# In the experts' first tile, the next tile's tokens are rounded behind the second weights, and the next first-layer weights behind the last part of the first layer

## The chip, the cores and the metric

The kernel runs on one core of a Trainium2 chip. The metric is device time in microseconds of one execution; the lowest is best. The kernel before was timed three times.

A core has five engines that work side by side, each through its own queue of instructions in order: PE (matrix multiplication; its weight loads are shown as PEld), DVE (vector work), ACT (activations, copies and casts), POOL (general work, and the issue of scatters) and SP, which here only issues loads. An instruction waits in its queue until what it needs is there, and everything behind it waits too.

## The reference

Attention over 8 batches of 8 heads, 576 tokens and head size 64, with a decay and a causal mask, and then a layer of 8 experts of which each token takes one:

```python
def _moe_ref(x, modality_id, w_gate, modality_bias, w1, w2):
    logits = x @ w_gate + modality_bias[modality_id]     # x: attention's output, 4608 x 512
    e_idx = np.argmax(logits, axis=1)
    ...                                                  # gate_w: the softmax weight of that expert
    for e in range(E):                                   # 8 experts
        mask = e_idx == e
        h = np.maximum(x[mask] @ w1[e], 0.0)             # 512 -> 1024
        out[mask] = gate_w[mask, None] * (h @ w2[e])     # 1024 -> 512
```

Everything is float32.

## The kernel before

**Attention** takes the first 395 us. It goes through the batches, and for each batch of tokens it works out the expert of each token and scatters its rows into per-expert lists in memory (`xs`); the scatters are issued by POOL (L769), five for each batch. The last batch's scatters are issued while the experts have already begun.

**The experts** (`Moe.run`) work through tiles of 256 tokens of one expert. To keep float32's accuracy, every operand of a matmul is split into a rounded part and the rest: ACT casts to the rounded part (names ending in h), and DVE subtracts it to get the rest (names ending in l). A product is then three matmuls: h with h, h with l, l with h. One tile has these steps:

- `load_x` (L1084): SP loads the tokens `xg` of tile t + 2. A load of tokens waits for all scatters recorded so far.
- `load_w1`, `load_w2`: SP loads raw weights of the next tile's expert into `raw1` and `raw2`. They are conditional: if the next tile has the same expert, nothing is moved.
- `split_w2`: four pieces of `w2h` (ACT, L1135) and `w2l` (DVE, L1136).
- `first` (L1160): the first layer in four groups of 24 matmuls, each into one PSUM bank `ph` of three; after each group ACT writes `hh` (L1171) and DVE `hl` (L1172).
- `split_w1`: four pieces of `w1h` (ACT, L1116) and `w1l` (DVE, L1118) of the next tile's weights. The q-th piece may only be overwritten when the q-th group of the first layer is done.
- `prepare` (L1143): PE transposes the next tile's `xg` in two halves into PSUM banks `px0` and `px1`; ACT casts to `xh` (L1155), DVE makes `xl` (L1156).
- `second` (L1180): the second layer, 24 matmuls for each half of the tokens, into `py0` and `py1`; DVE multiplies by the gate into `y` (L1190), and POOL scatters `y` to the output (L1191).

In what follows, a ph matmul is one of the first layer (128 x 128 by 128 x 256) and a py matmul one of the second (128 x 128 by 128 x 512).

After the first tile (`t == OTHERS`, which is 1), `other_tables` and `pads` run once: PE sums the counts of tokens (L971 and L1076, two small matmuls into `px0`), DVE copies them (`c_nb`, L975) and works out the tables of the remaining tiles, POOL writes padding rows (L1081).

**The order of the work.** A scheduler with its own model of durations places the instructions of the expert part on each engine; the program text only gives dependencies. In the first tile, which overlaps with the last of attention, some orders are fixed by hand: `self.order(x, behind)` says that instruction x stands behind another on its engine, without a wait. `follow(behind, x, y)` does so for a pair: x, an ACT instruction, behind `behind[0]`, and y, on DVE, behind `behind[1]`; it returns the pair's own names for the next. `split_w2` returns the four pairs of names (`w2h`, `w2l`); so `behind[3]` in `body` is the last pair. With `behind=None` nothing is fixed. After the last piece of w1 was ordered, the scheduler decides where the rest stands, on PE too, where no order is fixed by the lines that change.

Of the kernel before, what the change touches and what calls it, by code (L numbers as in the profile page):

```python
# [18 lines left out]
AF = mybir.ActivationFunctionType  # L19
# [41 lines left out]
def f32(ap):  # L61
    return ap.bitcast(F32)
# [132 lines left out]
class Attn:  # L195
# [303 lines left out]
    def max_mm(self, p, g):  # L499
        nc = self.nc  # L500
        X = self.get("X", p)
        self.owned(("cum", p % 3), p)
        pm = self.new(self.ps_s, "ps", ("m", p, g), [P, 2, 512], F32, 3)
        segs = self.SEG[g]
        masked = [s for s in segs if s[3] + s[1] == MW[s[2]]]
        first = True
        for c0, w, ic, j0 in masked:
            for x, n in ((0, P), (1, 64)) if w > 64 else ((1, 64),):
                for h in range(2):
                    r = slice(64 * h, 64 * h + 64)  # L510
                    nc.tensor.matmul(pm[:, h, c0 + w - n:c0 + w], self.id2[r, x], self.after[r, x, P - n:], start=first, stop=False,
                                     skip_group_check=True)
                first = False
        for c0, w, ic, j0 in segs:
            for h in range(2):
                r = slice(64 * h, 64 * h + 64)
                nc.tensor.matmul(pm[:, h, c0:c0 + w], self.Cq[r], self.Sk[r, p % 3, j0:j0 + w], start=not masked, stop=False,
                                 skip_group_check=True)
        for c0, w, ic, j0 in segs:
            for h in range(2):  # L520
                r = slice(64 * h, 64 * h + 64)
                nc.tensor.matmul(pm[:, h, c0:c0 + w], X[r, 0, QC - 64 + P * ic:QC + 64 + P * ic], X[r, 0, j0:j0 + w],
                                 start=False, stop=True, skip_group_check=True)
# [39 lines left out]
    def scores(self, p, g):  # L563
        nc = self.nc
        X = self.get("X", p)
        self.owned(("cum", p % 3), p)
        self.owned(("shift", p % 3), p)
        self.owned(("lo", p % 3), p)
        ps = self.new(self.ps_s, "ps", (p, g), [P, 2, 512], F32, 3)
        segs = self.KSEG[g]  # L570
        masked = [s for s in segs if s[3] == P * s[2]]
        first = True
        for c0, w, c, i0 in masked:
            for x, n in ((1, P), (0, 64)) if w > 64 else ((0, 64),):
                for h in range(2):
                    r = slice(64 * h, 64 * h + 64)
                    nc.tensor.matmul(ps[:, h, c0:c0 + n], self.id2[r, x], self.later[r, x, 0:n], start=first, stop=False,
                                     skip_group_check=True)
                first = False
        for c0, w, c, i0 in segs:  # L580
            k = slice(KC + P * c, KC + P * c + P)
            for h in range(2):
                r = slice(64 * h, 64 * h + 64)
                nc.tensor.matmul(ps[:, h, c0:c0 + w], self.Sk[r, p % 3, k], self.Sq[r, p % 3, 64 + i0:64 + i0 + w],
                                 start=not masked, stop=False, skip_group_check=True)
        for c0, w, c, i0 in segs:
            k = slice(KC + P * c, KC + P * c + P)
            q = slice(QC + i0, QC + i0 + w)
            for j, (x, y) in enumerate(((0, 0), (0, 1), (1, 0))):
                for h in range(2):  # L590
                    r = slice(64 * h, 64 * h + 64)
                    nc.tensor.matmul(ps[:, h, c0:c0 + w], X[r, x, k], X[r, y, q], start=False, stop=(j == 2), skip_group_check=True)  # L592
# [286 lines left out]
    def run(self, early=None):  # L879
        self.own("acc", -1)  # L880
        with self.tc.manual_schedule():
            self.setup(*self.begin)
            for s in self.steps(early).order():
                s["fn"]()
# [19 lines left out]
class Moe:  # L904
# [238 lines left out]
    def prepare(self, t, behind=None):  # L1143

        nc = self.nc
        xg = self.xg[t]
        xh = self.next("xh")
        xl = self.next("xl")
        self.xh[t], self.xl[t] = xh, xl
        for c in range(2):  # L1150
            px = (self.px(c) if t or c == 0 else self.next("ph")).rearrange("p (k n) -> p k n", n=P)
            for k in range(4):
                nc.tensor.transpose(px[:, k, :], xg[:, c, k * P:k * P + P], self.ident)
            a = xh[:, :, c * P:c * P + P]
            x = nc.scalar.copy(a, px)  # L1155
            y = nc.vector.tensor_tensor(xl[:, :, c * P:c * P + P], px, f32(a), ALU.subtract)  # L1156
            behind = self.follow(behind, x, y)
        return behind

    def first(self, t, ranks=None, behind=()):  # L1160
        nc = self.nc
        xh, xl = self.xh[t], self.xl[t]
        for g in range(4):
            ph = self.next("ph").rearrange("p (a n) -> p a n", a=2)
            for i in range(2):
                f0 = (2 * g + i) * P
                m = [(k, w, x) for k in range(4) for w, x in ((self.w1h, xh), (self.w1h, xl), (self.w1l, xh))]
                for j, (k, w, x) in enumerate(m):
                    y = nc.tensor.matmul(ph[:, i, :], w[:, k, f0:f0 + P], x[:, k, :], start=(j == 0), stop=(j == len(m) - 1))  # L1169
            a = self.hh[:, 2 * g:2 * g + 2, :]  # L1170
            nc.scalar.activation(a, ph, AF.Relu)  # L1171
            z = nc.vector.scalar_tensor_tensor(self.hl[:, 2 * g:2 * g + 2, :], ph, 0.0, f32(a), ALU.max, ALU.subtract)  # L1172
            if ranks:
                self.order(z, ranks[1] if g == 0 else behind[g - 1][1])
                if g:
                    self.order(behind[g][2], z.ins.name)
            if ranks and g == 2:
                self.order(ranks[0], y.ins.name)
# [60 lines left out]
    def run(self, acc, loads, behind, ahead, ranks):  # L1239
        self.load_w1(self.row[0], 0, loads)  # L1240
        self.load_w2()
        behind = self.split_w1(0, [0], behind, (0, 2))
        behind = self.prepare(0, behind)
        for x in ahead:
            self.order(x, behind[1])
        self.split_w1(0, [1, 2, 3], behind, (0, 2))
        self.nc.gpsimd.memset(self.raw1[1], 0.0)
        nest = ExitStack()
        for t in range(FULL):
            if t == OTHERS:  # L1250
                self.other_tables(self.counts(acc, self.px(0), "b", self.half_way))
                self.pads(acc)

            def body():
                self.load_w1(self.row[t + 1])
                if t + 2 < FULL:
                    self.load_x(t + 2)
                behind = self.split_w2(None if t else ranks)
                self.load_w2()
                self.first(t, None if t else ranks, behind)  # L1260
                self.split_w1(0, behind=None if t else behind[3])
                if t + 1 < FULL:
                    self.prepare(t + 1)
                half = self.second(self.xg[t], 2)
                if t == 0:
                    self.half_way = half
            if t == ALWAYS:
                every = ()
                nt = self.val(self.row[EARLY], 3, FULL - EARLY, ALWAYS - EARLY, every)
                nh = self.val(self.rowh[0], 3, 8, 0, every)  # L1270
                for h in range(2):
                    self.load_xh(h)
                self.prepare_h(0)
            if t >= ALWAYS:
                nest.enter_context(self.tc.If(nt > t - EARLY))
            body()
        nest.close()
        with ExitStack() as nest:  # L1278
            for t in range(8):
                nest.enter_context(self.tc.If(nh > t))  # L1280
                self.half(t)
# [85 lines left out]
```

## Time and profile before

| | |
|---|---|
| time, median of 3 runs | 873.17 us (872.64 to 876.27) |
| the profiled execution | 874.83 us, span of its instructions 873.0 us |
| mean granted PE clock | 0.989 |
| busy share of the span | PE 93%, PEld 84%, DVE 74%, ACT 60%, POOL 42% |
| attention | until about 395 us |
| the experts' first tile (t = 0) | about 382 to 420 us, overlapping with attention's end |
| tiles after that | some 23 us each |

The span is the time from the first to the last instruction on the core. In a row of the order of time stand the start, the duration, the engine, the line, the operation, what it writes and reads, and in brackets how long the engine had been idle and what ended that. In a row of the waits stand the waiting engine, its line, what it waited for, and then the sum in us, the number of waits, and the longest.

### The profile page before, as it was taken

How to read it: one execution, taken by the hardware profiler on the slowest of the kernel's cores; microseconds unless marked ns; L12 is line 12 of the kernel's file. 1: busy time of each engine (PE TensorE's matmuls, PEld its weight loads, DVE VectorE, ACT ScalarE, POOL GpSimd, SP SyncE). 2: the span in 40 equal slices, each digit the busy share in tenths (PEclk: the TensorE clock that was granted, in tenths of full speed). 3: DMA queues.
4: the chain of work that ended last, by engine and by line, in shares of the span. 5: the costliest groups of instructions: out<-in, count | busy, mean ns of one | idle time of the engine just before them, and what ended most of it. 6: DMA issues, size and time to landing. Idle time of an engine off the chain costs nothing. (4 is left out here: it accounts for less than half of the span.)

```text
span 873.0 us, 23522 instructions
## 1 busy us (share of the span) xinstructions
PE 814.1 (93%) x9702; PEld 731.2 (84%) x9702; DVE 649.2 (74%) x1214; ACT 521.3 (60%) x640; POOL 370.9 (42%) x346
## 2 busy tenths in 40 slices
PE   4899999999999999896999999999999999999894
PEld 3689888888888888785999999999999999999673
DVE  7789899999999999867876666666666656666394
ACT  3587777878787878564455445454445435455382
POOL 8366778888888888674510111111101100111010
PEclk9999999999999999999999999999999999999997
DMA  5334344444444443262267621101114321134650
GB/s 195 132 113 142 120 142 140 147 141 138 139 139 143 140 147 99 69 233 83 97 233 283 231 75 49 48 28 47 37 49 145 133 65 49 49 113 172 225 220 23
DMA packets 43301, 108.50 MB, mean 124 GB/s; under 512 B 5423, under 2 KB 5615, under 8 KB 43184
## 3 DMA queue, kind: packets, MB, share of 16 engines
q1 hardware_dynamic: 36480, 85.87, 29.5%
q0 software_dynamic: 6704, 21.02, 6.4%
q8 instruction: 79, 1.29, 0.6%
q14 instruction: 38, 0.31, 0.1%
HBM read 144.19 MB, written 21.80 MB: 190 GB/s over the span
## 5 line engine op out<-in xcount | busy, mean ns | idle before, releaser
L1191 POOL DMA_INDIRECT out_dram<-y,xg x36 | 45.8, 1272 | 352.4 <-DVE y L1190 335.2
L1169 PE MATMUL ph<-xh,w1h 128*128 128x256 f32 x576 | 163.1, 283 | 0.0
L1169 PE MATMUL ph<-xl,w1h 128*128 128x256 f32 x576 | 162.9, 283 | 0.0
L1169 PE MATMUL ph<-xh,w1l 128*128 128x256 f32 x576 | 162.9, 283 | 0.0
L1135 ACT CAST w2h<-raw 128x1024 fp32r<-128x1024 f32 x84 | 86.3, 1048 | 117.9 <-issue 57.4
L634 POOL TENSOR_TENSOR Pl<-Pt,Ph 128x1024 f16<-128x1024 f32 (+1 forms) x63 | 141.5, 2259 | 5.7 <-ACT Ph L622 5.3
L1136 DVE TENSOR_TENSOR w2l<-raw,w2h 128x1024 fp32r<-128x1024 f32 x84 | 100.5, 1220 | 52.2 <-ACT w2h L1135 50.8
L1118 DVE TENSOR_TENSOR w1l<-raw,w1h 128x1024 fp32r<-128x1024 f32 x78 | 96.1, 1240 | 56.9 <-ACT w1h L1116 56.5
L1116 ACT CAST w1h<-raw 128x1024 fp32r<-128x1024 f32 x80 | 83.0, 1048 | 90.3 <-PE ph L1169 67.1
L1186 PE MATMUL py<-w2l,hh 128*128 128x512 f32 x312 | 119.7, 393 | 2.7 <-DVE w2l L1136 2.7
L1186 PE MATMUL py<-w2h,hh 128*128 128x512 f32 x312 | 121.1, 397 | 0.0
L1186 PE MATMUL py<-w2h,hl 128*128 128x512 f32 x312 | 119.7, 392 | 0.0
L378 POOL TENSOR_TENSOR X<-raw,X 128x1216 fp32r<-128x1216 f32 x31 | 85.9, 2772 | 63.7 <-ACT X L372 60.6
L1169 PEld LDWEIGHTS ph<-xl,w1h 128*128 128x128 f32 x576 | 110.4, 192 | 0.8
L1169 PEld LDWEIGHTS ph<-xh,w1h 128*128 128x128 f32 x576 | 110.4, 192 | 0.7
L1169 PEld LDWEIGHTS ph<-xh,w1l 128*128 128x128 f32 x576 | 110.4, 192 | 0.0
L592 PE MATMUL ps<-X 64*128 64x288 f32 (+4 forms) x1152 | 106.9, 316 | 0.0
L660 PE MATMUL po<-vh,Ph 128*128 128x73 f16 x930 | 100.1, 198 | 6.4 <-DVE lgh L676 3.3
L607 ACT ACTIVATE Pt<-ps,lnp 128x576 f32<-128x576 f32 (+1 forms) x96 | 79.6, 866 | 43.6 <-PE ps L592 42.6
L660 PEld LDWEIGHTS <-Ph 128*128 128x128 f16 x960 | 93.7, 98 | 10.5 <-DVE lgh L676 4.7
L662 PE MATMUL po<-vh,Pl 128*128 128x73 f16 x930 | 99.8, 197 | 0.3 <-issue 0.3
L661 PE MATMUL po<-vl,Ph 128*128 128x72 f16 x930 | 99.9, 196 | 0.0
(285 smaller groups left out, 1888.7 us busy)
## 6 DMA issues: line engine op xcount, KB each, us to landing
raw<-in_w_dram SPq DMA_DIRECT2D x84, 1024.0 KB
raw<-in_qk_dram SPq DMA_DIRECT2D x32, 608.0 KB
xg<-xs SPq DMA_DIRECT2D x20, 514.0 KB
vT<-in_vt_dram SPq DMA_DIRECT2D x32, 320.0 KB
vr<-in_v_dram SPq DMA_DIRECT2D x30, 256.0 KB
raw1b<-in_w_dram SPq DMA_DIRECT2D x4, 1024.0 KB
hxg<-xs SPq DMA_DIRECT2D x5, 257.0 KB
vr<-in_v_dram SPq DMA_DIRECT2D x8, 128.0 KB
```

The source lines that it names most:

```text
L378: e.tensor_tensor(X[:, 1], self.get("raw", p), f32(X[:, 0]), ALU.subtract)
L592: nc.tensor.matmul(ps[:, h, c0:c0 + w], X[r, x, k], X[r, y, q], start=False, stop=(j == 2), skip_group_check=True)
L634: e.tensor_tensor(self.Pl_t[p % 2][:, :, c], self.exps(p, i), self.Ph_t[p % 2][:, :, c], ALU.subtract)
L660: nc.tensor.matmul(o, Ph[:, c0:c0 + P], vh[:, c, hh, :], start=(c == 0), stop=False)
L661: nc.tensor.matmul(o[:, 1:73], Ph[:, c0:c0 + P], vl[:, c, hh, :], start=False, stop=False)
L662: nc.tensor.matmul(o, Pl[:, c0:c0 + P], vh[:, c, hh, :], start=False, stop=(c == ic))
L1116: x = nc.scalar.copy(self.w1h[a], self.raw1[i][a])
L1118: y = e.tensor_tensor(self.w1l[a], self.raw1[i][a], f32(self.w1h[a]), ALU.subtract)
L1135: x = nc.scalar.copy(self.w2h[a], self.raw2[a])
L1136: y = nc.vector.tensor_tensor(self.w2l[a], self.raw2[a], f32(self.w2h[a]), ALU.subtract)
L1169: y = nc.tensor.matmul(ph[:, i, :], w[:, k, f0:f0 + P], x[:, k, :], start=(j == 0), stop=(j == len(m) - 1))
L1186: x = nc.tensor.matmul(py, h[:, k, c * P:c * P + P], w[:, k, :], start=(j == 0), stop=(j == len(m) - 1))
```

## The change

Three lines. In `prepare`, an order given by hand is applied to both halves of a tile's tokens only for tile 0; for another tile only to the second half (c = 1). `first` keeps the name of its last activation (`relu`). And in the body of the first tile, `split_w1` is ordered on ACT behind that activation instead of behind the last `w2h` cast (on DVE behind the last `w2l` as before), and `prepare` of tile 1, which had no order by hand, gets one: its second half stands behind the last `w2h` on ACT and behind the second `w2l` on DVE. For all later tiles nothing is said, as before.

```diff
             x = nc.scalar.copy(a, px)
             y = nc.vector.tensor_tensor(xl[:, :, c * P:c * P + P], px, f32(a), ALU.subtract)
-            behind = self.follow(behind, x, y)
+            if t == 0 or c == 1:
+                behind = self.follow(behind, x, y)
         return behind
...
             a = self.hh[:, 2 * g:2 * g + 2, :]
-            nc.scalar.activation(a, ph, AF.Relu)
+            self.relu = nc.scalar.activation(a, ph, AF.Relu).ins.name
...
                 self.first(t, None if t else ranks, behind)
-                self.split_w1(0, behind=None if t else behind[3])
+                self.split_w1(0, behind=None if t else (self.relu, behind[3][1]))
                 if t + 1 < FULL:
-                    self.prepare(t + 1)
+                    self.prepare(t + 1, None if t else (behind[3][0], behind[1][1]))
```

The scheduler's result differs on PE, DVE and ACT from the first tile on; the queues of POOL and SP are the same. One line is added, so that line numbers behind L1156 are one higher with the change. Names carry buffer numbers: `ph0` to `ph2` are the banks of the first layer, `py0` and `py1` of the second, `px00` and `px10` of the transposes, and `xh1`, `xl1` belong to tile 1.

**DVE**, first tile, after the last of attention's routing. Before:

```order
L738 TENSOR_REDUCE rr1_9328<-rrk_9324 128x5
L1156 TENSOR_TENSOR xl1_9409<-px10_9380,xh1_9407 128x4x128
L1136 TENSOR_TENSOR w2l_9435<-raw2_9399,w2h_9431 128x1024
L1172 SCALAR_TENSOR_TENSOR hl_9427<-ph2_9371,hh_9423 128x512
L1136 TENSOR_TENSOR w2l_9435<-raw2_9399,w2h_9431 128x1024
L1172 SCALAR_TENSOR_TENSOR hl_9427<-ph0_9369,hh_9423 128x512
L1136 TENSOR_TENSOR w2l_9435<-raw2_9399,w2h_9431 128x1024
L1172 SCALAR_TENSOR_TENSOR hl_9427<-ph1_9370,hh_9423 128x512
L1136 TENSOR_TENSOR w2l_9435<-raw2_9399,w2h_9431 128x1024
L1118 TENSOR_TENSOR w1l_9392<-raw1_9384,w1h_9388 128x4x256 x4
L1136 TENSOR_TENSOR w2l_9435<-raw2_9399,w2h_9431 128x1024
```

and with the change, from the fourth w2l on:

```order
L1136 TENSOR_TENSOR w2l_9435<-raw2_9399,w2h_9431 128x1024
L1118 TENSOR_TENSOR w1l_9392<-raw1_9384,w1h_9388 128x4x256 x4
L1156 TENSOR_TENSOR xl1_9409<-px10_9380,xh1_9407 128x4x128
L1136 TENSOR_TENSOR w2l_9435<-raw2_9399,w2h_9431 128x1024 x2
L1191 TENSOR_SCALAR y0_9410<-py0_9375,xg0_78 128x512
L1136 TENSOR_TENSOR w2l_9435<-raw2_9399,w2h_9431 128x1024
L1191 TENSOR_SCALAR y1_9411<-py1_9376,xg0_78 128x512
L975 COPY c_nb_9674<-px00_9365 1x8
```

The second half of tile 1's xl has moved from ahead of the first w2l to behind the four w1l; the first w2l follows the routing's reduction (L738) at once. What stands between, w2l and hl by turns, is unchanged.

**ACT**, at the same place, from the first tile's four w2h on. Before:

```order
L1135 CAST w2h_9431<-raw2_9399 128x1024 x4
L1116 CAST w1h_9388<-raw1_9384 128x4x256 x2
L1171 ACTIVATE hh_9423<-ph0_9369 128x512
L1155 CAST xh1_9407<-px10_9380 128x4x128
L1116 CAST w1h_9388<-raw1_9384 128x4x256 x2
L1171 ACTIVATE hh_9423<-ph1_9370 128x512
```

and with the change:

```order
L1135 CAST w2h_9431<-raw2_9399 128x1024 x4
L1172 ACTIVATE hh_9423<-ph0_9369 128x512
L1155 CAST xh1_9407<-px10_9380 128x4x128
L1172 ACTIVATE hh_9423<-ph1_9370 128x512
L1116 CAST w1h_9388<-raw1_9384 128x4x256 x4
L1135 CAST w2h_9431<-raw2_9399 128x1024 x4
```

All four w1h stand behind the last hh of the first layer, and xh1 two casts earlier.

**PE**, in the second layer of tile 0. Before, the transposes of tile 2's tokens (xg2) stand there, behind two matmuls of tile 1:

```order
L1186 MATMUL py1_9376<-w2h_9431,hh_9423 128x512
L1169 MATMUL ph2_9371<-xh1_9407,w1h_9388 128x256
L1169 MATMUL ph2_9371<-xl1_9409,w1h_9388 128x256
L1153 MATMUL px10_9380<-cident_61,xg2_80 128x128 x4
L1186 MATMUL py0_9375<-w2l_9435,hh_9423 128x512
L1186 MATMUL py0_9375<-w2h_9431,hl_9427 128x512
```

With the change xl1 is first used behind the whole second layer of tile 0 and the first count matmul:

```order
L1187 MATMUL py1_9376<-w2h_9431,hl_9427 128x512
L971 LDWEIGHTS cones_66
L971 MATMUL px00_9365<-c_acc_9347,cones_66 128x8
L1170 MATMUL ph1_9370<-xh1_9407,w1h_9388 128x256
L1170 MATMUL ph2_9371<-xl1_9409,w1h_9388 128x256
L1170 MATMUL ph2_9371<-xh1_9407,w1l_9392 128x256
```

and the first transpose of xg2 ahead of the last group of tile 1's first layer:

```order
L1170 MATMUL ph1_9370<-xh1_9407,w1h_9388 128x256
L1170 MATMUL ph1_9370<-xl1_9409,w1h_9388 128x256
L1170 MATMUL ph1_9370<-xh1_9407,w1l_9392 128x256
L1153 MATMUL px10_9380<-cident_61,xg2_80 128x128
L1170 MATMUL ph2_9371<-xh1_9407,w1h_9388 128x256
L1170 MATMUL ph2_9371<-xl1_9409,w1h_9388 128x256
```

The other three transposes of that half stand behind that group, after the four of the first half. The second count matmul (L1076) stands 37 ph matmuls behind the first use of xl1, and the transposes of xg2 32 more.

## The prediction

> **What bounds the kernel now.** I read the profile in this order: busy time by stretch, the waits of the matmul engine, then the order of time around each wait. First the stretches round the hand-over from attention to the experts (columns: stretch, length, then PE, PEld, DVE, ACT, POOL busy, granted clock, DMA share, GB/s).
>
> ```profile
> 400.00:410.00 10.00, 3.52 (x16) 2.79 (x17) 10.00 (x11) 3.15 (x4) 7.15 (x6) 1.00 0.43 159
> 410.00:420.00 10.00, 10.00 (x42) 8.06 (x41) 5.46 (x7) 2.85 (x4) 1.00 (x1) 0.83 0.06 26
> 420.00:440.00 20.00, 20.00 (x136) 18.49 (x136) 16.23 (x65) 7.54 (x10) 11.27 (x9) 1.00 0.31 119
> 440.00:500.00 60.00, 60.00 (x407) 55.72 (x406) 39.94 (x43) 31.42 (x38) 6.79 (x6) 1.00 0.70 251
> ```
>
> From 410 to 500 PE is never idle, and DVE, ACT and DMA have room: the expert part runs at PE's pace, so PE time lost at its start goes straight into the end. It loses some: only 3.52 of the 10 us before 410, and a granted clock of 0.83 in the next 10. Two of PE's waits lie there.
>
> ```profile
> PE px L1153 <- DMA xg<-xs: 4.9, 1, 4.9
> PE py L1186 <- DVE w2l L1136: 2.7, 1, 2.7
> ```
>
> In order of time (start, duration, instruction), with the rows that give the pace between them:
>
> ```profile
> 398.49 0.28 PE L1169 MATMUL ph<-xl,w1h 128*128 128x256 f32 x1
> 398.61 0.28 PE L1169 MATMUL ph<-xh,w1l 128*128 128x256 f32 x1
> 401.62 0.50 PE L1186 MATMUL py<-w2l,hh 128*128 128x512 f32 x1 [2.73 <-DVE w2l L1136]
> 401.96 0.39 PE L1186 MATMUL py<-w2h,hl 128*128 128x512 f32 x1
> ...
> 404.62 0.28 PE L1169 MATMUL ph<-xl,w1h 128*128 128x256 f32 x1
> 409.76 0.78 PE L1153 MATMUL px<-cident,xg 128*128 128x128 f32 x4 [4.86 <-DMA xg<-xs]
> 410.19 0.78 PE L1186 MATMUL py<-w2l,hh 128*128 128x512 f32 x1
> ...
> 413.67 0.39 PE L1186 MATMUL py<-w2l,hh 128*128 128x512 f32 x1
> 413.90 0.39 PE L1186 MATMUL py<-w2h,hl 128*128 128x512 f32 x1
> ```
>
> Starts count here, as matmuls overlap: a ph matmul takes 0.12 us (398.49 to 398.61), a py matmul 0.23 (413.67 to 413.90). After the second wait eight py matmuls take 3.48 us (410.19 to 413.67).
>
> **What the change takes away.** In tile 0 the second half of tile 1's rounding (xh, then xl) no longer stands ahead of the first w2l on DVE, and ACT casts w1h only after the whole first layer. The scheduler's PE order follows: xl of tile 1 and the transposes of tile 2's tokens (xg) come later.
>
> First wait. DVE's side of it:
>
> ```profile
> 396.19 0.20 DVE L738 TENSOR_REDUCE rr<-rrk 128x5 f32<-128x40 f32 x1
> 399.75 0.69 DVE L1156 TENSOR_TENSOR xl<-px,xh 128x512 fp32r<-128x512 f32 x1 [3.36 <-ACT xh L1155]
> 400.36 1.22 DVE L1136 TENSOR_TENSOR w2l<-raw,w2h 128x1024 fp32r<-128x1024 f32 x1
> 401.49 0.68 DVE L1172 SCALAR_TENSOR_TENSOR hl<-ph,hh 128x512 fp32r<-128x512 f32 x1
> 402.09 1.22 DVE L1136 TENSOR_TENSOR w2l<-raw,w2h 128x1024 fp32r<-128x1024 f32 x1
> ...
> 406.69 4.62 DVE L1118 TENSOR_TENSOR w1l<-raw,w1h 128x1024 fp32r<-128x1024 f32 x4
> 420.70 0.75 DVE L1190 TENSOR_SCALAR y<-py,xg 128x512 f32<-128x512 f32 x1
> 421.36 0.14 DVE L975 COPY c_nb<-px 1x8 f32<-1x8 f32 x1
> ```
>
> DVE stands idle 3.36 us for xh, which ACT does late; PE waits for the w2l behind it. With xl gone from there w2l can start at 396.4 and end at 397.6, before PE asks at 398.73 (398.61 + 0.12). PE gains 401.62 - 398.73 = 2.89, and 0.11 of a slow first interval (401.62 to 401.96 is 0.34 instead of 0.23): 3.00 us.
>
> Second wait. PE asks for xg's transposes at 404.74 and starts at 409.76: 5.02 us. In the new order 34 py matmuls and much of tile 1's first layer stand ahead of them. The eight slow matmuls go with the wait: 3.48 - 8 x 0.23 = 1.64. The sum is 3.00 + 5.02 + 1.64 = 9.66 us.
>
> **Whether the work ahead is ready.** The new PE clock, counted from 398.73: 12 py (2.76) to 401.5, one ph, 12 py to 404.4, one ph, 22 py (5.06) to 409.6, one count matmul and one ph, xl first used at 409.7, 37 ph (4.44) to the second count matmul at 414.2, 32 ph (3.84) to the first transpose of xg at 418.0. Against it ACT and DVE, from these rows and those above:
>
> ```profile
> 394.86 1.99 ACT L1135 CAST w2h<-raw 128x1024 fp32r<-128x1024 f32 x2
> 396.75 2.00 ACT L1116 CAST w1h<-raw 128x1024 fp32r<-128x1024 f32 x2
> 398.65 0.59 ACT L1171 ACTIVATE hh<-ph 128x512 fp32r<-128x512 f32 x1
> 399.14 0.58 ACT L1155 CAST xh<-px 128x512 fp32r<-128x512 f32 x1
> 399.60 2.00 ACT L1116 CAST w1h<-raw 128x1024 fp32r<-128x1024 f32 x2
> 407.32 1.05 ACT L1135 CAST w2h<-raw 128x1024 fp32r<-128x1024 f32 x1 [5.21 <-DMA raw<-in_w_dram]
> ```
>
> - ACT: hh at 396.75, xh to 397.7, then hh of the last group when PE ends it at 398.9, to 399.5; four w1h at 0.95 each end at 403.4. The first, done at 400.6, is wanted at 401.5; the second (401.5) at 404.4; the third (402.4) at 409.6. So the later w1h is hidden, by 0.9 us at the narrowest.
> - DVE: w2l (1.13) and hl (0.60) by turns from 396.4 to 402.7, always ahead of their matmuls; four w1l (4.6) to 407.3; xl to 407.9, wanted at 409.7: 1.8 us to spare.
> - Behind xl in DVE's queue stand tile 1's w2l, y, the count copy c_nb, and hl. w2l waits for ACT's w2h, whose wait ends at 407.32 as before: two casts to 409.2, a third, once py1's fifth of eleven is done at 408.5, to 410.2. DVE: two w2l from 408.4 to 410.7, y (0.66) to 411.3, w2l to 412.5, y to 413.1, c_nb to 413.25; the second count matmul wants that at 414.2: 0.9 us to spare. The next hl frees a bank of PSUM for PE's group at 418.0: ACT's w1h after the ph group that ends at 412.5 is done at 413.7, DVE's last w2l and six small copies (0.08 each) end at 414.9, w1l at 416.0, two small ones and hl at 416.9: 1.1 us to spare.
> - The tokens xg land unchanged before 409.76; wanted at 418.0.
>
> That 407.32 hangs on POOL and SP, where nothing is moved:
>
> ```profile
> 381.15 0.91 POOL L769 DMA_INDIRECT xs<-x,rde  x1 [0.21 <-issue]
> ...
> 406.44 3.52 POOL L1247 MEMSET raw1b<- 128x4096 f32 x1 [2.29 <-DMA xs<-x,rde]
> 406.45 0.36 SPq L1089 DMA_DIRECT2D xg<-xs  x1
> 407.16 0.51 SPq L1110 DMA_DIRECT2D raw<-in_w_dram  x2
> ```
>
> The last scatter of tokens lands at 406.44; SP then loads xg and issues raw at 407.16, and ACT starts 0.16 us later, so that load is skipped (tile 1 has tile 0's expert). Then DVE's queue can't run ahead of the scatters, and the slack of 0.9 us is all there is.
>
> **Costs that the trace doesn't show.** Splitting xg's transposes into two pieces on PE: between 0 and 0.1 us (the transposes' whole stretch was 0.43, 409.76 to 410.19); I take 0.06. The first w2l's real readiness is hidden behind xl: somewhere from below 396.4 to 400.36. Beside raw it waits, as the program has it, for five scatters of the seventh image, the last issued at 381.15; with the landing of 2.29 us above that is 384.4, so I take 396.4; the other end costs 3.0 us. DVE beside POOL:
>
> ```profile
> 385.28 2.97 POOL L1118 TENSOR_TENSOR w1l<-raw,w1h 128x1024 fp32r<-128x1024 f32 x1 [0.50 <-ACT w1h L1116]
> 386.77 2.56 DVE L1118 TENSOR_TENSOR w1l<-raw,w1h 128x1024 fp32r<-128x1024 f32 x1
> ```
>
> A w1l of DVE took 2.56 instead of 1.22 beside such an operation of POOL, +1.34. Now four w2l shift onto POOL's scatters and xl, w2l onto its memset. The price is between 0 (w2l at 400.36 and 402.09 took 1.22 during scatters, four w1l at 406.69 took 4.62 during the memset) and 4 x 1.34 = 5.4 us of DVE. I take 0, as those rows are the same pair of operations. Nothing here can gain: PE does the same matmuls.
>
> [...]
>
> So the span goes from 873.0 to 873.0 - 9.6 = 863.4. The profiled execution took 874.83, 1.83 more than its span, and lies above the median of 873.17; from the median I forecast **863.5 us**.
>
> **Rivals.**
> 1. *A new wait on DVE takes part of it back.* If the four w2l run beside POOL at 2.56, DVE is 5.4 us late, xl ends at 413.3, and PE waits 3.6 at 409.7, a gap longer than the 2.73 that left the clock alone, shorter than the 4.86 that didn't. With the slow matmuls (1.64) 5.2 is lost: 868.7; for smaller stretches, beyond 0.9 us of slack, 864 to 867. [...]
> 2. *The first w2l isn't ready.* It would start at 400.36 as now: 3.0 us less, 866.5. For it: its own wait was never seen. Against: 384.4.
> 3. *The loads take it back.* From 440 the queue moves 251 GB/s; if loads set the pace there, tiles 3 on would not start earlier, and the time stays at 873.
>
> ```profile
> SPq L1097 <- DVE w1l L1118: 25.2, 10, 5.4
> ACT w1h L1116 <- DMA raw<-in_w_dram: 0.2, 1, 0.2
> ```
>    Against: from 330 to 560 SP's weight loads wait for DVE, and after 440 ACT waits for a load 0.2 us in all: loads follow compute.
> 4. *Slower: xl at the end of DVE's queue.* If all eight operations ahead of it (four w2l, four w1l) ran at 2.56, xl would end 10.7 us late, at 418.6; PE would stand 8.9 us at 409.7 and pay 1.64: 873.17 - 9.6 + 10.5 = 874.1. It decides from xl ending at 417.7. Against: the 4.62 for four w1l.
>
> **Chances.** Forecast 0.73; rival 1 0.13; rival 2 0.06; rival 3 0.05; rival 4 0.03. About 0.5% (4.4 us) is what a measurement tells from no change. The forecast, rival 2 and most of rival 1 are beyond it: faster 0.91; rival 3 and rival 1's extreme within: 0.06; slower 0.03. The range: 862.0, since the lowest of the runs shown (872.64) less 9.66 is 863.0 and a microsecond is left for scatter; up to 868.7 with rival 1's extreme.
>
> **What would show it.** Right: w2l starts near 396.5 without a wait; PE has no wait over 0.5 us from 398 to 440 and the granted clock of that stretch is 1.00; the first transposes of xg start near 418; the count copy ends near 413. Wrong: a PE wait for xl, c_nb or hl between 409 and 419 (rival 1 or 4), w2l starting near 400 (rival 2), or ACT waiting for raw after 430 with PE idle (rival 3).

## The result, and the profile after

The changed kernel took **869.23 us** (median of 11 runs, 865.85 to 872.75); the kernel before, run beside it, 875.35 us (11 runs, 870.88 to 878.74). The ratio is 0.9937, with a 95% interval of 0.991 to 0.9963: faster by 5.5 us by that ratio, where 9.6 were forecast. The forecast of 863.5 is not reached, and 869.23 lies above the upper end of the range, 868.7. A part of that distance is the kernel before, which took 2.2 us more here than the 873.17 from which the forecast started; the gain itself fell short all the same.

The profiled execution took 870.31 us, with a span of 868.6 against 873.0. First the stretches after the hand-over, and PE's waits from 396 to 500 (columns as in the prediction):

```profile
400.00:410.00 10.00, 10.00 (x47) 8.03 (x46) 8.46 (x9) 3.72 (x4) 7.84 (x9) 1.00 0.34 119
410.00:420.00 10.00, 6.81 (x51) 6.70 (x51) 6.98 (x14) 5.51 (x7) 5.26 (x2) 0.91 0.23 80
420.00:440.00 20.00, 20.00 (x120) 18.08 (x120) 15.36 (x59) 7.07 (x10) 11.09 (x10) 0.96 0.37 128
```

```profile
PE px L1076 <- DVE c_nb L975: 3.2, 1, 3.2
```

The stretch from 400 to 410, where PE was busy for 3.52 us before, is full now, at clock 1.00. Both waits of the prediction are gone. But a new one stands between 410 and 420, and the clock falls behind it. In order of time on PE:

```profile
414.48 0.28 PE L1170 MATMUL ph<-xh,w1l 128*128 128x256 f32 x1
417.95 0.17 PE L1076 MATMUL px<-c_acc,cones 128*128 128x8 f16 x1 [3.19 <-DVE c_nb L975]
...
418.30 0.41 PE L1170 MATMUL ph<-xh,w1l 128*128 128x256 f32 x1
...
421.50 0.37 PE L1170 MATMUL ph<-xh,w1h 128*128 128x256 f32 x1
```

PE could have gone on at 414.60 (414.48 + 0.12) and does at 417.95: 3.35 us. From 418.30 to 421.50 lie 15 ph matmuls at 0.213 us instead of 0.12: 1.40 us. Lost together: 4.75 of the 9.66 that were to be won, which leaves 4.9.

That sum can be held against the trace without what varies elsewhere. I measure the **expert part** on PE: from the matmul L724 of the last routing to the end of the last full tile, which is the start of the first half tile's matmul (L1223 before, L1224 after) less the idle time in its bracket.

```profile
395.65 0.18 PE L724 MATMUL pb<-acc,ones 128*128 128x40 f16 x1
...
818.76 0.47 PE L1223 MATMUL ph<-w1h,hxh 128*128 128x512 f32 x1 [2.86 <-issue]
```

```profile
396.06 0.18 PE L724 MATMUL pb<-acc,ones 128*128 128x40 f16 x1
...
814.44 0.76 PE L1224 MATMUL ph<-w1h,hxh 128*128 128x512 f32 x1 [2.97 <-PEq L1278]
```

Before: 818.76 - 2.86 - 395.65 = 420.25. After: 814.44 - 2.97 - 396.06 = 415.41. That is 4.84 less, against 4.9 from the sum. So the three terms of the forecast came together as predicted, and a new wait took half of them back.

Where that wait comes from is read on POOL. Its scatters and the small operation ahead of them, before and then after (start, duration):

```profile
396.54 0.20 POOL L742 TENSOR_TENSOR re<-re,rr 128x5 f32<-128x5 f32 x1 [1.38 <-DVE rr L738]
397.47 0.98 POOL L769 DMA_INDIRECT xs<-x,rde  x1 [0.32 <-POOL between L768]
398.76 1.01 POOL L769 DMA_INDIRECT xs<-x,rde  x1 [0.22 <-issue]
400.07 0.97 POOL L769 DMA_INDIRECT xs<-x,rde  x1 [0.21 <-issue]
401.35 1.06 POOL L769 DMA_INDIRECT xs<-x,rde  x1 [0.22 <-issue]
402.72 1.43 POOL L769 DMA_INDIRECT xs<-x,rde  x1 [0.22 <-issue]
```

```profile
396.94 1.24 POOL L742 TENSOR_TENSOR re<-re,rr 128x5 f32<-128x5 f32 x1 [1.38 <-DVE rr L738]
398.86 1.85 POOL L769 DMA_INDIRECT xs<-x,rde  x1 [0.27 <-POOL between L768]
401.02 1.45 POOL L769 DMA_INDIRECT xs<-x,rde  x1 [0.21 <-issue]
402.78 1.39 POOL L769 DMA_INDIRECT xs<-x,rde  x1 [0.21 <-issue]
404.47 1.97 POOL L769 DMA_INDIRECT xs<-x,rde  x1 [0.21 <-issue]
406.75 1.97 POOL L769 DMA_INDIRECT xs<-x,rde  x1 [0.23 <-DMA xs<-x,rde]
```

The five scatters take 8.63 us instead of 5.45, and L742 takes 1.24 instead of 0.20: 4.22 us more in a row. What follows them is late by that and by 0.40, by which attention's routing ended later in this execution (L724 at 396.06 instead of 395.65). SP and ACT after:

```profile
411.09 0.36 SPq L1089 DMA_DIRECT2D xg<-xs  x1
411.79 0.51 SPq L1110 DMA_DIRECT2D raw<-in_w_dram  x2
```

```profile
411.94 3.89 ACT L1135 CAST w2h<-raw 128x1024 fp32r<-128x1024 f32 x4 [8.23 <-DMA raw<-in_w_dram]
```

SP issues xg at 411.09 instead of 406.45, 4.64 later, and raw behind it. ACT's w2h, to which the prediction gave 407.32, waits 8.23 us and starts at 411.94. Then DVE:

```profile
396.90 1.23 DVE L1136 TENSOR_TENSOR w2l<-raw,w2h 128x1024 fp32r<-128x1024 f32 x1
398.04 0.68 DVE L1173 SCALAR_TENSOR_TENSOR hl<-ph,hh 128x512 fp32r<-128x512 f32 x1
398.64 1.22 DVE L1136 TENSOR_TENSOR w2l<-raw,w2h 128x1024 fp32r<-128x1024 f32 x1
...
403.24 4.62 DVE L1118 TENSOR_TENSOR w1l<-raw,w1h 128x1024 fp32r<-128x1024 f32 x4
407.78 0.68 DVE L1156 TENSOR_TENSOR xl<-px,xh 128x512 fp32r<-128x512 f32 x1
413.02 2.36 DVE L1136 TENSOR_TENSOR w2l<-raw,w2h 128x1024 fp32r<-128x1024 f32 x2 [4.56 <-ACT w2h L1135]
...
417.75 0.14 DVE L975 COPY c_nb<-px 1x8 f32<-1x8 f32 x1
```

DVE itself is not slowed: w2l 1.22, four w1l 4.62, xl done at 408.5 with time to spare, all as predicted. It then stands idle for 4.56 us behind tile 1's w2l, and the count copy c_nb ends at 417.89 instead of 413.25.

### The profile page after: what moved, and what is told of

Its sections match the earlier page's. It is cut to its first block, busy times and chain, and to the rows that moved or that the text cites. A ratio compares the mean times of both kernels' runs of the same rounds, so it can differ in the third digit from the quotient of the medians.

```text
span 868.6 us, 23523 instructions
## 1 busy us (share of the span) xinstructions
PE 813.0 (94%) x9702; PEld 731.4 (84%) x9702; DVE 648.8 (75%) x1214; ACT 520.4 (60%) x640; POOL 374.9 (43%) x346
```

## The experiments

The numbers are those of the order in which they were run; they are told by question. Each ratio is against runs of the kernel before on the same chip. The table at the end has the expert part of all.

**1. Does the wait run through SP's order?** In the first tile SP issues the raw weights ahead of the tokens xg, so that they no longer stand behind the scatters. The orders on PE, DVE and ACT stay.

```
-                self.load_w1(self.row[t + 1])
-                if t + 2 < FULL:
+                if t != 1:
+                    self.load_w1(self.row[t + 1])
+                if t and t + 2 < FULL:
                     self.load_x(t + 2)
...
                 self.split_w1(0, behind=None if t else (self.relu, behind[3][1]))
+                if t == 0:
+                    self.load_w1(self.row[2])
+                    self.load_x(2)
```

> The changed kernel, with one thing more: in the first tile SP issues the second tile's w2 load and the third tile's w1 load ahead of the load of tile 2's tokens (xg), which waits for attention's last scatters. The order on PE, DVE and ACT is that of the changed kernel. Theory (the changed kernel's new wait of 3.2 us at the second count matmul comes down the line scatters, xg load, raw w2 load, w2h, w2l, c_nb): the first w2h of tile 1 starts near 404 instead of 411.9, c_nb ends near 413, PE does not wait from 398 to 440, the granted clock there is 1.00, and the time is 9 to 10 us under the kernel before (ratio 0.989). Rival (DVE's queue itself, or ACT, is too slow for PE's new order): c_nb is still late, a wait of 2 to 3 us stays at the second count matmul, ratio near 0.994 as with the change.

Measured: 863.38 us (6 runs, 861.16 to 869.73), ratio 0.989 (0.9851 to 0.9929). SP, DVE, and the whole stretch from 396 to 440:

```profile
410.66 0.36 SPq L1089 DMA_DIRECT2D xg<-xs  x1
```

```profile
412.40 0.14 DVE L975 COPY c_nb<-px 1x8 f32<-1x8 f32 x1
```

```profile
396.00:440.00 44.00, 44.00 (x285) 39.93 (x284) 36.52 (x87) 21.01 (x27) 29.07 (x26) 1.00 0.35 124
```

xg is as late as in the change (410.66), the scatters are as long (1.85, 1.45, 1.40, 1.97, 1.96), and it costs nothing: c_nb is early, and PE is busy for all 44 us at clock 1.00. The lateness reaches PE only through the raw load behind xg.

**2. Is it DVE's work beside the scatters that stretches them?** w1 of tile 1 is not rounded in tile 0 (`if t: self.split_w1(0)`). This leaves out four w1h and four w1l; tile 1 then works with tile 0's rounded weights, which are the same expert's.

> The changed kernel without the rounding of tile 1's first-layer weights (four w1h on ACT, four w1l on DVE); tile 1 has tile 0's expert, so the rounded weights of tile 0 stay in use. Theory (POOL's scatters are stretched by DVE operations with two operands in SBUF that run beside them): the first two scatters still take 1.4 to 1.9 us beside w2l, the third to fifth, now free of w1l, about 1.0 to 1.2 instead of 1.4, 2.0, 2.0; the load of xg is issued near 409 instead of 411.1, c_nb ends near 415.6, the wait at the second count matmul shrinks from 3.2 to about 1 us with no slow clock behind it; ratio 0.989 to 0.991. Rival (the scatters are stretched by something other than DVE, such as the DMA rings): all five stay at 1.4 to 2.0, xg is issued near 411 and the wait stays at 3.2.

Measured: 866.73 us (10 runs, 863.62 to 870.63), ratio 0.9915 (0.9891 to 0.9938). The last two scatters, which ran beside w1l in the change:

```profile
403.88 0.97 POOL L769 DMA_INDIRECT xs<-x,rde  x1 [0.22 <-issue]
405.16 0.97 POOL L769 DMA_INDIRECT xs<-x,rde  x1 [0.21 <-issue]
```

They are back at 0.97, and PE's wait falls to 1.4 us, with no slow stretch behind it. The third stayed at 1.39, where I had expected 1.0 to 1.2: it started beside the last w2l.

**3. and 4. The halves of the change.** In experiment 3 only w1h is moved behind the whole first layer, and `prepare` stays without an order. In experiment 4 only `prepare` is ordered behind w2l.

```
experiment 3:
-                    self.prepare(t + 1, None if t else (behind[3][0], behind[1][1]))
+                    self.prepare(t + 1)
experiment 4:
-                self.split_w1(0, behind=None if t else (self.relu, behind[3][1]))
+                self.split_w1(0, behind=None if t else behind[3])
```

> Only one half of the change: the second tile's w1 behind the last part of the first layer; the order of the tokens' rounding as in the kernel before, so that xl of tile 1 stands ahead of the first w2l on DVE again and the transposes of xg stand early on PE again. Both theories: xh comes two casts earlier, xl starts near 398 instead of 399.75, and PE's first wait shrinks from 2.9 to about 1 us. Theory of the stretched scatters: w2l and w1l come 2 us earlier onto the scatters, which end 1 to 3 us later than before, xg lands near 411 to 412, and PE's wait for it grows from 4.9 to 7 or 8 us: the time is 0 to 2.5 us above the kernel before (ratio 1.000 to 1.003). Rival (scatters not stretched by DVE): xg lands at 409.8 as before, the time is that of the kernel before (ratio 1.000) with the scatters at 1.0 to 1.4.

Measured: 875.03 us (12 runs, 871.4 to 879.26), ratio 1.0013 (0.9989 to 1.0038). PE's waits from 396 to 440:

```profile
PE px L1153 <- DMA xg<-xs: 8.6, 1, 8.6
PE py L1187 <- DVE w2l L1136: 0.8, 1, 0.8
```

The first wait is 1.9 shorter and the second 3.7 longer: w2l starts at 399.21 instead of 400.36, falls onto more scatters (0.98, 1.80, 1.40, 1.43, 1.43), and xg is issued 1.8 us later after routing (12.57 us after L724 instead of 10.80), while PE asks for it 1.9 us earlier.

> Only the other half of the change: the tokens' rounding behind w2; w1h stays where it was on ACT (two casts ahead of hh and xh). The orders on PE and DVE come out as in the changed kernel. Theory: DVE runs the same operations over the scatters at the same times, the wait at the second count matmul is 3 us as with the change; ratio 0.993 to 0.995, so this half is the whole of the change. Rival (the place of w1h matters too): ACT's hh of the last groups come 2 us later, PE waits for hl or hh in the second layer of tile 0, and the time is 1 to 2 us above the changed kernel's.

Measured: 866.08 us (9 runs, 863.53 to 870.09), ratio 0.9911 (0.9885 to 0.9938). The rival, that w1h ahead of hh costs PE time, fell: this half is the whole gain. But it is more than I had expected (ratio 0.993 to 0.995, a wait of 3 us). Its hh is late for DVE, though, and the pause shows what the scatters need. DVE, then POOL:

```profile
401.82 0.69 DVE L1173 SCALAR_TENSOR_TENSOR hl<-ph,hh 128x512 fp32r<-128x512 f32 x1 [0.95 <-ACT hh L1172]
```

```profile
402.06 0.97 POOL L769 DMA_INDIRECT xs<-x,rde  x1 [0.21 <-issue]
```

A scatter that starts beside hl, one operand of which is in PSUM, takes 0.97, and PE's wait for c_nb is 2.2 us instead of 3.2. So moving w1h, the other half of the change, gives nothing back: it closes that pause.

**What holds a scatter.** I set attention's last five scatters of each of the 13 traces, 65 in all, against the operation that DVE was running when they started. Where that was a w2l or w1l (53), the scatter ended 0.83 to 0.88 us after the end of that operation, in every case. In the change: w2l 398.64 to 399.86, scatter to 400.71; the w2l at 400.37 ends at 401.59, scatter to 402.47. The kernel before shows it twice in rows that stand above: the w2l at 400.36 ended at 401.58 and the scatter of 401.35 at 402.41; the w2l at 402.09 ended at 403.31 and the scatter of 402.72 at 404.15. Where DVE was idle, or ran xl or hl (12), a scatter took 0.97 to 1.01. So these scatters were held until the one operation ended; they did not run at a reduced rate. L742 ends 0.05 us after w2l does.

The kernel before shows the same far from this place. Of its 39 scatters of the output (L1191), 18 started under a w2l, took 1.12 to 1.78 us and ended 0.85 to 0.87 after it; 20 started while DVE was idle and took 0.98 to 1.00. But "the one operation" is not the whole rule. In the trace of experiment 8 a scatter of the output took 5.12 us:

```profile
828.97 5.12 POOL L1192 DMA_INDIRECT out_dram<-y,hxg  x1 [12.88 <-DMA raw<-in_w_dram]
```

The scatter at the same place in the trace of the change took 1.71: it started at 830.79, 0.36 us into the first of four w2l in a row (830.43, 1.21), and ended 0.86 after that first one. To end 0.86 after the fourth it would have taken 4.62 - 0.36 + 0.86 = 5.12, so I estimate that four held the other, with 4.62 for four of them as elsewhere. The four w1l of the first tile follow each other as closely, and a scatter there was held by one of them alone (404.47 in the change, ended 0.85 after the w1l of 404.38). Why four would hold the other was not settled.

**5. Is it the second operand?** w1l is made from w1h alone, times 0, four operations at the same place. This leaves out the low part of tile 1's first-layer weights.

```
-            y = e.tensor_tensor(self.w1l[a], self.raw1[i][a], f32(self.w1h[a]), ALU.subtract)
+            y = e.tensor_scalar(self.w1l[a], f32(self.w1h[a]), 0.0, None, ALU.mult)
```

> The changed kernel, but in tile 0 DVE makes each w1l from w1h alone (w1h times 0) and no longer from raw and w1h: one operand in SBUF instead of two, the same place in DVE's order. This leaves out the low part of tile 1's first-layer weights. Theory (POOL's scatters stretch only beside DVE operations with two operands in SBUF): the first three scatters stay at 1.85, 1.45, 1.39 us, since the w2l beside them are untouched; the fourth and fifth fall from 1.97 to 0.97, as they did when no w1l stood there; xg is then issued near 408.5 and PE's wait at the second count matmul is 1.2 to 1.6 us without a slow stretch. Rival (any large DVE operation on SBUF stretches them): the fourth and fifth stay at 1.9 to 2.0 and the wait at 3 us.

Measured in one run: 865.19 us. DVE, then POOL:

```profile
402.57 2.75 DVE L1118 TENSOR_SCALAR w1l<-w1h 128x1024 fp32r<-128x1024 f32 x4
```

```profile
403.80 1.03 POOL L769 DMA_INDIRECT xs<-x,rde  x1
404.82 0.52 POOL L768 MEMSET between<- 1x1 int32 x1
405.13 1.02 POOL L769 DMA_INDIRECT xs<-x,rde  x1
```

By the times my theory had won: 1.03 and 1.02, a wait of 1.4. But the operations are shorter too, 0.68 to 0.81 us instead of 1.22, and both scatters started within the last 0.2 us of one; the memset beside them grew from 0.09 to 0.52. Each ends 0.84 or 0.85 us after that operation does, as if held by it. By the times alone the run doesn't tell "one operand doesn't hold" from "one operand holds, but briefly". Hence:

**10. One long operation of one operand** (128x4096 in place of four), with the same part left out.

> The changed kernel, but in tile 0 one DVE operation makes all of w1l from w1h alone (128x4096, times 0): one operand in SBUF, one long operation of some 2.7 us in place of four. This leaves out the low part of tile 1's first-layer weights. Theory (a scatter that starts while DVE runs an operation that reads and writes SBUF alone, with one operand or two, is held until that operation ends and takes 0.85 us more): the scatter that starts within this operation ends 0.85 us after the operation's end, so that it takes up to 3.5 us, more than any so far. Rival (only operations with two operands in SBUF hold it, and the 1.03 and 1.02 us beside four short ones were chance): it takes 0.97 to 1.0 us.

Measured in one run: 872.38 us. DVE, then POOL:

```profile
405.35 2.51 DVE L1123 TENSOR_SCALAR w1l<-w1h 128x4096 fp32r<-128x4096 f32 x1 [0.43 <-ACT w1h L1116]
```

```profile
406.07 2.63 POOL L769 DMA_INDIRECT xs<-x,rde  x1
```

The operation ends at 407.86, the scatter at 408.70: 0.84 later. My theory of experiment 5 falls: this multiplication with one operand holds a scatter too. Not every operation on SBUF with one operand holds POOL's work. In attention L742 runs beside a reduction (am, L398) that reads one operand in SBUF, and takes its 0.20, where it took 1.24 beside w2l. DVE, then POOL, from the kernel before:

```profile
99.37 1.21 DVE L398 TENSOR_REDUCE am<-vr 128x1 f32<-128x1024 f32 x1
```

```profile
99.60 0.20 POOL L742 TENSOR_TENSOR re<-re,rr 128x5 f32<-128x5 f32 x1 [0.90 <-DVE rr L738]
```

**11. Halves of w1l.** If a scatter is held by one operation, then smaller ones hold it for less. Each w1l of tile 0 is made by two operations of 128x512; nothing is left out.

```
+            for h in range(2):
+                a = (slice(None), slice(None), slice(q * 256 + h * 128, q * 256 + h * 128 + 128))
                 y = e.tensor_tensor(self.w1l[a], self.raw1[i][a], f32(self.w1h[a]), ALU.subtract)
```

> The changed kernel with each w1l of tile 0 made by two DVE operations of half the size (128x512) in a row; nothing is left out, the rest of the order stays. Theory (held until the end of the one operation that runs at the scatter's start): the fourth and fifth scatters are held at most 0.6 us instead of 1.1 and take 0.85 to 1.47 us instead of 1.97; xg is issued 1 to 2.2 us earlier, PE's wait for c_nb falls from 3.2 to between 1 and 2.2 us, and the kernel is 1 to 3.5 us faster than the change, ratio 0.989 to 0.992. Rival (POOL and DVE share a rate, so that only the bytes that DVE moves beside a scatter count): both scatters stay at 1.9 to 2.0 us and the wait at 3 us or more.

Measured: 868.39 us (6 runs, 865.03 to 870.75) beside 875.73, ratio 0.9915 (0.9892 to 0.9937). The last two scatters, and PE's wait:

```profile
403.18 1.50 POOL L769 DMA_INDIRECT xs<-x,rde  x1 [0.22 <-issue]
...
404.99 1.50 POOL L769 DMA_INDIRECT xs<-x,rde  x1 [0.21 <-issue]
```

```profile
PE px L1076 <- DVE c_nb L975: 1.9, 1, 1.9
```

1.50 instead of 1.97, a little over the 1.47 that I gave as the upper end, and the wait is 1.3 us shorter. Of that, 0.9 us is the scatters' (8.63 to 7.70 for all five); for the rest PE asks 0.36 us later after routing, as the scheduler placed the rest of PE's work anew. Shared rates would have left both as they were, since DVE moves the same bytes.

**6. and 7. Are the terms of the sum separate?** Experiment 6 is the kernel before with the edit of experiment 1 on SP alone; experiment 7 is experiment 4 with that edit.

> The kernel before, with the same edit on SP alone (raw's loads for tile 1 and tile 2 issued ahead of xg of tile 2); the rounding order on DVE and ACT for the first layer stays as it was, and the scheduler puts the transposes of xg late on PE by itself. Theory (the two waits are separate terms): the wait for xg and the slow matmuls behind it go, 5.02 + 1.64 = 6.66; the wait for the first w2l behind xl stays at 2.7 us. Span 873.0 - 6.6 = 866.4, ratio 0.9925. Rival (one wait hides in the other, so that either edit brings all of it): no wait at w2l either, span 863, ratio 0.989. Rival (xg late has no part in it, the order of DVE does it all): a wait of 4 us or more is left between 404 and 420, ratio above 0.997.

Measured: 868.2 us (12 runs, 865.86 to 873.71) beside 874.01, ratio 0.9942 (0.992 to 0.9965). The only wait of PE from 396 to 440:

```profile
PE py L1186 <- DVE w2l L1136: 2.7, 1, 2.7
```

The expert part is 6.77 us shorter, against 5.02 + 1.64 = 6.66 from the prediction's second and third terms. The first, the wait of 2.7 us, is left whole.

> The transposes' half of the change alone (w1h on ACT as before, tile 1's xh and xl and tile 2's transposes late), with the edit on SP. Theory (with SP's order out of the way nothing on PE's path hangs on the scatters, so that DVE's pause for hh no longer matters): no PE wait over 0.5 us from 396 to 440, PE busy all 44 us at clock 1.00, span 862 to 863, ratio 0.989 as with the whole change and the same SP edit. Rival (w1h behind the first layer costs time of its own, so that its half alone is 2 us faster here too): span near 860.3, ratio 0.987.

Measured: 866.24 us (6 runs, 863.68 to 867.69), ratio 0.9907 (0.9876 to 0.9937), no wait of PE in that stretch. The span is 864.0, above the 862 to 863 that I had expected. The expert part is 8.64 shorter, against 9.08 in experiment 1: the rival, that the w1h half costs 2 us of its own, fell.

**8. and 9. The change, and the change with the edit on SP, on one chip.**

> The changed kernel as it is, beside the same with the edit on SP, on one chip, to have the two against the same runs of the kernel before. From the traces: the expert part (from the last matmul of routing to the end of the last full tile on PE) was 4.84 us shorter than before with the change (420.25 to 415.41). Theory (the new wait for c_nb and the slow matmuls behind it are lost in every run): about 4.8 us faster, ratio 0.9945. Rival (they belong to that one profiled run, and most runs have the whole gain): 9.6 us, ratio 0.989, the same as its neighbour here.

> The change with the edit on SP again, on the same chip as the change alone. From the traces its expert part was 9.08 us shorter than before (420.25 to 411.17). Theory: 9 us faster than before, ratio 0.9896, and 4 to 5 us faster than the change alone. Rival (the difference between the two was the chip or the runs): the two ratios lie within 0.2% of each other.

Measured: the change 867.84 us (7 runs, 865.44 to 870.6), ratio 0.9933 (0.991 to 0.9957); with the edit on SP 863.86 us (6 runs, 860.25 to 868.45), ratio 0.9904 (0.9874 to 0.9935); the kernel before 873.87 us. The intervals overlap, the traces do not leave it open:

| | PE's wait, 396 to 440 (us) | five scatters (us) | expert part (us) | against before |
|---|---|---|---|---|
| before | 2.7 and 4.9 | 5.45 | 420.25 | |
| the change | 3.2 | 8.63 | 415.41 | -4.84 |
| 8, the change again | 3.1 | 8.63 | 415.33 | -4.92 |
| 1, SP's order | none | 8.63 | 411.17 | -9.08 |
| 9, the same again | none | 8.63 | 410.59 | -9.66 |
| 2, no w1 rounding | 1.4 | 6.63 | 412.16 | -8.09 |
| 3, w1h moved alone | 0.8 and 8.6 | 7.04 | 422.43 | +2.18 |
| 4, tokens moved alone | 2.2 | 7.40 | 414.37 | -5.88 |
| 5, w1l of one operand | 1.4 | 6.74 | 412.17 | -8.08 |
| 6, before with SP's order | 2.7 | 5.46 | 413.48 | -6.77 |
| 7, experiment 4 with SP's order | none | 7.40 | 411.61 | -8.64 |
| 10, one long w1l | 3.2 | 8.29 | 415.39 | -4.86 |
| 11, w1l in halves | 1.9 | 7.70 | 414.15 | -6.10 |

The change with SP's order has the shortest expert part of all that compute everything. On one chip it beats the change by a nominal 4 us of time and by 4.7 us of expert part (415.33 to 410.59). Two traces of one kernel differ by 0.08 us of expert part (the change) or 0.58 (with SP's order), so differences of that size mean nothing.

## Why the prediction was wrong

- **First wait, second wait, slow matmuls: 3.00 + 5.02 + 1.64.** Right: both waits are gone from the change, experiment 6 took the last two terms alone (6.77 for 6.66), and where nothing else comes in the way nearly the whole 9.66 appears: 9.08 in experiment 1 and 9.66 in experiment 9, the same kernel twice. That the second agrees to the last digit is luck.
- **The first w2l ready at 396.4.** Right: it starts at 396.90 behind rr, without a wait, and rr is 0.4 us later than before. Rival 2 fell.
- **"That 407.32 hangs on POOL and SP, where nothing is moved."** This is the step that failed: that the start of tile 1's w2h would stay where it was. Nothing was moved on POOL, but DVE's work was moved onto it in time. L742 and the scatters took 4.22 us longer, the load of raw came behind them, and w2h started at 411.94. That cost PE the 4.75 us: the wait of 3.35 for c_nb and 1.40 at the slow clock.
- **DVE beside POOL, from 0 to 5.4 us.** I priced it at 0 from rows of DVE: w2l and w1l keep their 1.22 beside scatters. They do. The price falls on the other side, and I had the rows for it: the scatters of 401.35 (1.06) and 402.72 (1.43) were the two that started under a w2l, and they ended 0.83 and 0.84 after it. With that rule the new order gives the 3.2 us of the scatters; the 1.04 of L742 stood in no row of before, where DVE was idle beside it or ran the reduction am. Of the 4.22 together the slack of 0.9 us that I had worked out leaves 3.3, and 3.35 were lost, then 1.40 at the slow clock. The slack was right, and so was the place.
- **Rival 1** was right in the wait (DVE's queue, at c_nb), and wrong in which engine is stretched: it had DVE late and PE waiting for xl. Its time, "864 to 867" for smaller stretches, had left out that a wait of 3.2 us can pay the slow clock; it gave 1.64 only to the extreme, a wait of 3.6 us. No run shows that only so long a wait pays it: 1.91 (experiment 11) and 2.18 us (experiment 4) paid too, and 2.73 (before) did not. The 4.75 us that were lost come to 868.3 on that scale (863.5 + 4.75), close to its extreme of 868.7.
- **Which side is held.** The scatters: 53 that started under a w2l or w1l ended 0.83 to 0.88 us after it. The runs don't show a scatter holding DVE in turn: four w1l took 4.62 us beside scatters (403.24 in the change), as they did with no scatter beside them (406.69 before).
- **Rivals 3 and 4** fell: no loads took time back (the expert part is 4.84 us shorter, where the sum leaves 4.9), and in the change PE waited for c_nb alone from 396 to 500, not for xl.

## What to carry to other kernels

When work is moved in time on one engine, look at what it will now run beside on the others, and read the rows of both sides: a price of 0 on DVE says nothing of the price on POOL. Here a vector operation of the kinds of w2l and w1l (1.22 us in the change) delayed a scatter of POOL by what was left of it: 53 scatters ended 0.83 to 0.88 us after the one they started under. Halves of w1l delayed it less (1.50 instead of 1.97); xl and hl, each with an operand in PSUM, did not (0.97). The scatter of 5.12 us shows that this is not the whole rule. And where a short slack hangs on a queue in which one instruction waits for something late (here xg ahead of raw on SP), taking that instruction out of the way can be worth more than making the late thing less late: here 4.2 to 4.7 us of expert part for one edit, against 1.2 to 1.3 for halving w1l.

## What the runs showed that I had not expected

- **A slow clock does not follow from a wait's length alone.** After waits of 2.73 (before) and 2.7 us (experiment 6) there was none: the granted clock is 1.00 from 401.60 to 409.70 before, and from 396 to 440 in experiment 6. After 1.91 (experiment 11), 2.18 (experiment 4) and 3.19 us (the change) there was one, of 3.2 us by the matmuls' starts (the granted clock from 418.30 to 421.70 in the change is 0.50), and it came later behind the shorter waits: from 416.6 when PE had gone on at 415.74 (experiment 11), and from 417.4 in experiment 4, whose rows these are, with the first and last of the slow matmuls near them:

```profile
416.21 0.17 PE L1076 MATMUL px<-c_acc,cones 128*128 128x8 f16 x1 [2.18 <-DVE c_nb L975]
...
417.63 0.42 PE L1170 MATMUL ph<-xh,w1l 128*128 128x256 f32 x1
...
420.41 0.41 PE L1170 MATMUL ph<-xh,w1h 128*128 128x256 f32 x1
```

  What decides it was not settled. The prediction's reading, that of rival 1's waits only the extreme would pay, did not hold.
- **PE's wait ahead of the first half tile is 1.1 to 1.3 us in some executions and 2.9 to 3.3 in others** (2.86 before, 2.97 in the change), and it differs for one kernel too: 3.09 in experiment 1 and 1.19 in experiment 9. So it does not come from the change, and it is why spans alone would have misled: 873.0 - 868.6 = 4.4 and 867.9 - 858.5 = 9.4 for pairs whose expert parts differ by 4.84 and 4.74.
